# A transformer block on one core: pair 1 by seven block products, z1 of the last tiles behind the change of memory

## The chip, the cores and the metric

The kernel runs on one core of a Trainium2 chip. Its time is the device time of one execution in microseconds. Five engines work side by side, each through its own queue in the order in which the program wrote it: TensorE (PE, matmuls; its weight loads are listed apart as PEld), VectorE (DVE), ScalarE (ACT), GpSimd (POOL) and SyncE (SP), which here issues all DMA transfers. They wait for each other by semaphores.

## The reference

One block on 2048 tokens of width 512, all in float32: a linear-attention half and a gated-MLP half, each behind a layer norm whose scale and shift come from a condition vector `c`.

```python
mod = (silu(c) @ w_mod).reshape(1, 6, 1, -1)          # sa, ca, ga, sb, cb, gb
h = layernorm(x) * (1 + ca) + sa
x = x + ga * A(h, wqkv, wo)                           # linear attention, 32 heads of 16
h = layernorm(x) * (1 + cb) + sb
x = x + gb * B(h, w_in, w_sp, b_sp, w_out)

def B(x, w_in, w_sp, b_sp, w_out):                    # F = 1376, Fh = 688
    z = gelu(x @ w_in)
    z1 = z[..., :Fh]
    z2 = layernorm(z[..., Fh:])
    g = einsum("ts,bsf->btf", w_sp, z2) + b_sp        # 2048 x 2048 by 2048 x 688
    return (z1 * g) @ w_out
```

## The kernel before

Tokens are cut into 16 tiles of 128. Every product is made exact enough by splitting both factors into a high and a low part: the high part is a rounded copy (always on ACT), the low part is the difference (on DVE or POOL), and three matmuls are summed (high by high, high by low, low by high). So each operand costs ACT one pass and DVE or POOL another.

The order of the work is written out by hand. `ORDER` and `ORDER3` are strings of words such as `z013`, operation `z0` for tile 13, and `run_all` (L560) issues them one after the other; each word appends its instructions to the queues of the engines that it uses. What comes earlier in the string comes earlier in each queue. The buffers are chosen by hand as well: `SLOTS` gives for each kind of tile the buffer that its next use takes.

`ORDER` has two parts that flow into each other. The first makes K, Q and the sums of linear attention: weights `wk`, `wq` are built from loaded pieces (`lw` loads, `mr` mean products, `wf` DVE, `qh` high part on ACT, `qd` and `qg` low part on DVE and POOL), x tiles come as they are (`lx`, statistics `s1`) and transposed (`ly`, split by `th`, `tl`), and `kk`, `km`, `qm`, `gm` are the matmuls. The second part works tile by tile: attention output `wo`, residual and statistics `x1`, normalised `h2`, its transpose by DMA (`hp` planes on ACT and transfer, `hm` merge on DVE, `hh`, `hl` split), then two products with `w_in`: `z0` (z1, 24 matmuls of 344 columns, L650) and `z1` (z2, the same), gelu on ACT (`g1`, `g2`), z1 written to memory (in `g1`), z2 normalised (`zl` statistics on DVE with a power op on POOL, `zn` on ACT with its bias `zb` on DVE, L672), parked in memory (`zp`) and split (`zh` on ACT, `zo` on POOL, L686).

Then the memory changes hands: the pools `ws`, `ta`, `tb` and the PSUM pools are closed (L836), and those of the second half are laid over them. `ws` holds `w_in`, so z1 and z2 products come ahead of this point. The last modulation vector (`mB5`, evacuated on ACT at L240) stands directly ahead of it.

`ORDER3` makes `w_sp @ z2`. w_sp is loaded half a row tile at a time (`lh`, 512 KB). Token tiles are taken in pairs. Pairs 2 to 7 use a block scheme that takes seven products in the place of eight: the four blocks of a pair's w_sp give sums (`ss`, DVE, L899 to L908), those are split (`fh` ACT, `fl` DVE, `fg` POOL, L915 and L918), the z2 tiles give differences (`ts` loads the parked z2, `td` DVE) that are split (`th`, `tl`), `pr` p,h,k is one of seven products over eight token tiles (12 matmuls, L928), and `cs`, `cd` add up the results. Pair 0 is done plainly (`aH`, `aL` split w_sp, `pp` t,k is 24 matmuls, `ce` ends). Pair 1 is mixed: its first half (h = 0) by blocks, its second half plainly (`pp2,2 pp2,3 pp3,2 pp3,3`), summed into the same PSUM banks by the table `MIX`.

The result `us` of a tile is multiplied by z1 (`um`, z1 read back by `lz`), cut into 16-bit planes (`up`, two ACT copies), transposed by DMA (`ux`), merged (`ug`, two DVE copies at L278), written to memory (`uq`), read back (`ur`), split (`uh`, `ul`) and multiplied by `w_out` (`wm`, 17 matmuls of 512 columns), and added to the residual (`ot`).

Of the kernel before, what the change touches and what calls it, by code (L numbers as in the profile page):

```python
# [26 lines left out]
def block_kernel(ctx: ExitStack, tc: tile.TileContext, x, x_t, w_qkv, w_o, w_in, w_sp, b_sp, w_out,  # L27
# [641 lines left out]
    def z2_norm(t):  # L669
        z = ZZ[t]  # L670
        b = sm([P, 1], "zb")
        nc.vector.scalar_tensor_tensor(b, MEAN["z", t], -1.0, RSTD["z", t], op0=OP.mult, op1=OP.mult)  # L672
        nc.scalar.activation(z, z, AF.Identity, scale=RSTD["z", t], bias=b)
# [11 lines left out]
    def z2_lo(t):  # L685
        nc.gpsimd.tensor_sub(Z2[t][:, 1], ZZ[t], f(Z2[t][:, 0]))  # L686
# [84 lines left out]
    def hx_lo(t):  # L771
# [19 lines left out]
        yp0,0 yp0,1 wf0,0 wf0,2 kk1,1 kk1,2 yp0,2 kk0,2 kk0,3 lx5 th2 lm0,3 yp0,3 lx2 ya0,1 ya0,2 kk1,3 tl2  # L791
        ya0,3 cr0 qh0,1 qh0,0 qg0,0 lx1 wf0,3 qh0,3 s11 qd0,1 kr0 km2 qh0,2 qg0,2 ce0 bp0 kr1 by0 ly5 s12 kr2
        bp1 qd0,3 bp2 qm0 ba1 by1 by2 ba2 by3 bx1 lo1 th5 qr0 tl5 bp3 ba3 qm1 qr1 bb1 s15 be1 ka0 lM2 ly8 bh2
        bl2 bh0 bl0 k20 k40 km5 k15 qm2 ly3 bx0 lx3 bb0 kh0 kl0 gm0 ka1 th3 tl3 km3 qm3 s13 th8 bh1 bl1 ly4
        lo0 th4 be0 q12 ka2 q22 mV2,0 lx4 mV2,1 ks0 q42 kr3 tl4 k22 k42 km4 k21 k41 li qm5 lw2,0 vh1 ks1 kh1
        q13 ly6 k25 s14 k14 k45 qm4 kh2 ly9 th9 kl2 mS2 kl1 th6 tl6 k24 ka3 mB2 k23 bh3 gm1 tl9 q14 tl8 k43
        bl3 q15 lx6 q24 lx9 ks2 ks3 kh3 qa0 k44 ks4 s16 s19 ks5 lx8 kh4 km8 vh0 wg3 s18 km6 k16 bh9 bh5 bl5
# [375 lines left out]
```

## Time and profile before

| | |
|---|---|
| median of 3 runs | 623.13 us (622.82 to 623.35) |
| the profiled execution's own time | 622.78 us |
| its span, first to last instruction | 621.0 us |
| PE busy | 611.8 us, 3371 matmuls |
| DVE busy | 486.7 us, 907 instructions |
| ACT busy | 334.9 us, 576 instructions |
| POOL busy | 221.5 us, 185 instructions |
| DMA | 105.75 MB, 170 GB/s mean |

The profile is that of one execution. Times are counted from its first instruction. A row of a group reads: line, engine, operation, tiles written and read with their shape, count, then busy us and the mean ns of one, then the engine's idle time just before these instructions and what ended most of it. In a timeline the first two numbers are start and duration in us, and the bracket gives the idle time before it and what released it. Matmuls overlap: each lasts longer than the step from one to the next, so their steps and not their durations tell their cost.

### The profile page before, as it was taken

Reading aid. Unit: us, or ns where it says so; the run is one execution under the profiler, and the core shown is the slowest. Engines: PE = TensorE matmul, PEld = TensorE weight load, DVE = VectorE, ACT = ScalarE, POOL = GpSimd, SP = SyncE. Lnnn points to the kernel's source line nnn. Section 1 sums busy time; section 2 is a strip of 40 time slices with the busy share of each in tenths; the row PEclk is TensorE's granted clock in tenths of the full one; section 3 lists DMA queues with packets and bytes.
Section 4 is the critical chain, followed back from the end, with each engine's and each line's share of the span. In section 5 each row is a group of like instructions: output and inputs, shape, how many; then the busy total and the mean of one; then the engine's idle time right before and its main releaser. Section 6 shows DMA issues by size and latency. Waiting matters only on the chain.

```text
span 621.0 us, 9510 instructions
## 1 busy us (share of the span) xinstructions
PE 611.8 (99%) x3371; PEld 557.5 (90%) x3371; DVE 486.7 (78%) x907; ACT 334.9 (54%) x576; POOL 221.5 (36%) x185
## 2 busy tenths in 40 slices
PE   8999999999999999999999999999999999999997
PEld 6688888888799999999999999999999999998886
DVE  2899989888788988787776599997867786886651
ACT  2778678565556667565536365454454453543420
POOL 0843434635866577364252420232122121300000
PEclk9999999999999999999999999999999999999999
DMA  8454313260244667566734866652586555989962
GB/s 274 155 203 134 103 69 103 65 207 20 84 119 116 164 180 185 173 194 181 209 127 159 316 252 129 203 178 68 172 201 192 150 182 145 288 266 254 292 224 77
DMA packets 91023, 105.75 MB, mean 170 GB/s; under 512 B 57088, under 2 KB 57600, under 8 KB 90976
## 3 DMA queue, kind: packets, MB, share of 16 engines
q1 hardware_dynamic: 90976, 105.15, 56.1%
q8 instruction: 26, 0.43, 0.3%
q14 instruction: 21, 0.17, 0.1%
HBM read 66.07 MB, written 25.95 MB: 148 GB/s over the span
## 4 chain that ended last, share of the span: by engine, by line
PE 83%; DVE 6%; DMA 4%; issue 3%; POOL 1%; SPq 1%; ACT 1%; POOLq 0%; DVEq 0%; ACTq 0%
PE P L928 23%; PE z L650 16%; PE Pq L928 5%; PE pout L112 3%; PE pout L110 3%; PE pout L111 3%; PE kp L111 2%; PE kp L112 2%; PE kp L110 2%; PE g L110 2%; PE g L112 2%; PE g L111 2%; PE qp L112 2%; PE qp L111 2%; PE qp L110 2%
## 5 line engine op out<-in xcount | busy, mean ns | idle before, releaser
L650 PE MATMUL z<-win,ht 128*128 128x344 f32 x768 | 122.9, 320 | 0.2 <-DVE ht L298 0.2
L650 PEld LDWEIGHTS z<-win,ht 128*128 128x128 f32 x768 | 121.4, 188 | 1.3 <-DVE ht L298 0.5
L928 PE MATMUL P<-z,f 128*128 128x344 f32 x624 | 102.7, 320 | 0.0
L928 PEld LDWEIGHTS P<-z,f 128*128 128x128 f32 x624 | 99.0, 188 | 0.1
L918 POOL TENSOR_TENSOR f<-raw_wsp,f 128x512 fp32r<-128x512 f32 x26 | 37.2, 1441 | 138.9 <-ACT f L915 135.5
L254 POOL TENSOR_TENSOR mv<-ve,mhalf 128x1 f32<-128x1 f32 x48 | 36.6, 765 | 58.6 <-DVE ve L253 52.2
L915 ACT ACTIVATE f<-raw_wsp 128x512 fp32r<-128x512 f32 x52 | 31.8, 626 | 29.9 <-PE P L928 14.9
L915 ACT ACTIVATE f<-sa 128x512 fp32r<-128x512 f32 x39 | 24.3, 629 | 34.1 <-DVE sa L905 11.2
L918 DVE TENSOR_TENSOR f<-sa,f 128x512 fp32r<-128x512 f32 x39 | 28.5, 741 | 10.7 <-ACT f L915 10.6
L470 POOL TENSOR_TENSOR pksum<-pksum,tk 128x512 f32<-128x512 f32 x15 | 22.2, 1483 | 40.8 <-DVE tk L442 40.8
L112 PE MATMUL pout<-wout,ut 128*128 128x512 f32 (+1 forms) x85 | 32.4, 382 | 0.0
L110 PE MATMUL pout<-wout,ut 128*128 128x512 f32 (+1 forms) x85 | 32.4, 381 | 0.0
L111 PE MATMUL pout<-wout,ut 128*128 128x512 f32 (+1 forms) x85 | 32.3, 380 | 0.0
L928 PE MATMUL Pq<-z,wsp 128*128 128x344 f32 x192 | 30.9, 322 | 0.9 <-ACT mod L240 0.9
L686 POOL TENSOR_TENSOR z<-zz,z 128x688 fp32r<-128x688 f32 x16 | 28.8, 1817 | 8.0 <-ACT z L683 5.2
L928 PEld LDWEIGHTS Pq<-z,wsp 128*128 128x128 f32 x192 | 30.4, 188 | 1.3 <-ACT mod L240 1.3
L1023 ACT ACTIVATE ut<-ur 128x384 fp32r<-128x384 f32 x32 | 15.3, 518 | 24.2 <-DMA ur<-ud 15.1
L268 ACT COPY uca<-us 128x768 uint16<-128x768 uint16 x32 | 25.0, 828 | 5.2 <-PE P L928 3.6
L579 POOL TENSOR_TENSOR prod<-pq,zrep 128x512 f32<-128x512 f32 x16 | 21.2, 1335 | 15.1 <-ACT zrep L705 4.1
L110 PE MATMUL kp<-wk,ht 128*128 128x512 f32 x64 | 25.8, 403 | 0.0
L111 PE MATMUL kp<-wk,ht 128*128 128x512 f32 x64 | 25.4, 396 | 0.2 <-DVE wk L343 0.2
L110 PE MATMUL g<-pkhl,hhl 128*128 128x512 f32 x64 | 25.3, 396 | 0.0
(257 smaller groups left out, 1546.3 us busy)
## 6 DMA issues: line engine op xcount, KB each, us to landing
raw_wsp<-in_w_sp SPq DMA_DIRECT2D x32, 512.0 KB, 4.7
ud<-uca SPq DMA_DIRECT2D x16, 384.0 KB, 3.4
ur<-ud SPq DMA_DIRECT2D x16, 384.0 KB, 4.1
z1d<-z SPq DMA_DIRECT2D x16, 344.0 KB, 2.3
zd<-zz SPq DMA_DIRECT2D x16, 344.0 KB, 3.0
z1r<-z1d SPq DMA_DIRECT2D x16, 344.0 KB, 3.8
xt<-in_x_t SPq DMA_DIRECT2D x16, 256.0 KB, 3.8
x<-in_x SPq DMA_DIRECT2D x16, 256.0 KB, 2.6
```

The source lines that it names most:

```text
L110: mm(o, a_hi, b_hi, start=first, stop=False, **kw)
L111: mm(o, a_hi, b_lo, start=False, stop=False, **kw)
L112: mm(o, a_lo, b_hi, start=False, stop=last, **kw)
L254: nc.gpsimd.tensor_tensor(mv[:, 1:2], ve, mhalf, op=OP.pow)
L268: nc.scalar.copy(pl[:, h], v[:, :, h])
L470: nc.gpsimd.tensor_add(pksum, pksum, PK[t])
L579: nc.gpsimd.tensor_mul(pr, PQ[t], KV["z"])
L650: mm(p[:, b, :HB], a[:, i, kc], win[h][:, j, kc, b * HB:(b + 1) * HB], start=kc == 0 and k == 0, stop=kc == KC - 1 and k == 2)
L686: nc.gpsimd.tensor_sub(Z2[t][:, 1], ZZ[t], f(Z2[t][:, 0]))
L915: nc.scalar.activation(SF[p, h, k][:, 0], s_src(p, h, k), AF.Copy)
L918: eng.tensor_sub(SF[p, h, k][:, 1], s_src(p, h, k), f(SF[p, h, k][:, 0]))
L928: mm(B[key][:, :HB], a[:, x_], b[:, y_], start=i == 1, stop=i == n)
```

## The change

Five things, and a new `ORDER`, `ORDER3` and `SLOTS` around them.

- The z1 products of tiles 12 to 15 (`z012` to `z015`, `g112` to `g115`) leave `ORDER`. `ORDER3` has `zw` (the same 24 matmuls, into two single banks) and `zg` (gelu in two halves of 344 columns, then the write to memory) in their place.
- Pair 1's second half goes by blocks too: `pp2,2 pp2,3 pp3,2 pp3,3` and their splits go; `ss1,1`, `fh1,1`, `fl1,1`, `fg1,1`, `pr1,1` come, `MIX` goes, and pair 0 uses banks 4 to 7.
- `ug` copies on ACT in the place of DVE.
- `zo`, the low part of z2, is on DVE for tiles 11 to 15.
- The bias `zb` has another form, with one tensor operand in the place of two.

The K weight is loaded in four pieces (`lk`) in the place of two (`lw1`).

```diff
-        nc.vector.scalar_tensor_tensor(b, MEAN["z", t], -1.0, RSTD["z", t], op0=OP.mult, op1=OP.mult)
+        nc.vector.tensor_scalar(b, MEAN["z", t], RSTD["z", t], -1.0, op0=OP.mult, op1=OP.mult)
...
-        nc.gpsimd.tensor_sub(Z2[t][:, 1], ZZ[t], f(Z2[t][:, 0]))
+        (nc.gpsimd if t < 11 else nc.vector).tensor_sub(Z2[t][:, 1], ZZ[t], f(Z2[t][:, 0]))
...
+    def z_late(t):
+        ZB[t, 0] = [bank(2 * (t % 2) + b, f"z0{b}_{t}") for b in range(2)]
+        a = HT2[t]
+        for kc in range(KC):
+            for k, (i, j) in enumerate(((0, 0), (0, 1), (1, 0))):
+                for b in range(2):
+                    mm(ZB[t, 0][b][:, :HB], a[:, i, kc], win[0][:, j, kc, b * HB:(b + 1) * HB],
+                       start=kc == 0 and k == 0, stop=kc == KC - 1 and k == 2)
+
+    def z1_late(t):
+        z = sb("st", [P, 2, HB], F32, f"z1_{t}")
+        for b, p in enumerate(ZB.pop((t, 0))):
+            nc.scalar.activation(z[:, b], p[:, :HB], AF.Gelu_apprx_tanh)
+        Z1D[t] = dram.tile([P, FH], F32, tag=f"z1d{t}", name=f"z1d{t}")
+        dma(Z1D[t], z.rearrange("p a b -> p (a b)"))
...
-    MIX = {(2, 0): ((1, 2), 4, 36), (2, 1): ((1, 3), 5, 36), (3, 0): ((1, 4), 6, 36), (3, 1): ((1, 0), 7, 24)}
-
     def prod(p, h, k):
-        n = 24 if p > 1 else 36 if k in (2, 3, 4) else 12
         for j in range(4):
-            chain((p, k), BANK[k], n, SF[p, h, k][:, :, j], t_of(4 * h + j, k))
+            chain((p, k), BANK[k], 24, SF[p, h, k][:, :, j], t_of(4 * h + j, k))
 
     def plain(t, k):
         for s in range(4):
             for h in range(2):
-                key, where, n = (("q", t, h), 2 * t + h, 3 * NT) if t < QUAD else MIX[t, h]
-                chain(key, where, n, WSP[t, k][:, :, s], Z2[4 * k + s][:, :, h * HB:(h + 1) * HB])
+                chain(("q", t, h), 4 + 2 * t + h, 3 * NT, WSP[t, k][:, :, s], Z2[4 * k + s][:, :, h * HB:(h + 1) * HB])
...
-            if p == 1:
-                nc.vector.tensor_add(U[t1][:, HI], B[p, 0][:, :HB], U[t1][:, HI])
...
-        merge(UC[t][1], UC[t][0].rearrange("p a b -> p (a b)").rearrange("p (a b) -> p a b", b=2))
+        merge(UC[t][1], UC[t][0].rearrange("p a b -> p (a b)").rearrange("p (a b) -> p a b", b=2), nc.scalar.copy)
...
     ORDER = """
-        lm1,0 si lm1,1 du1 du2 du3 du4 cm1,0 cm1,1 lm1,2 lm1,3 lw1,0 cm1,2 cm1,3 mc du5 mr1,0 lw1,1 ly1 th1
-        tl1 ly0 lw0,0 th0 tl0 mr1,1 mr1,2 mr1,3 ce1 wf1,3 qh1,3 mr0,0 lm0,1 lw0,1 mr0,1 mr0,2 mr0,3 qg1,3
-        wf1,1 qh1,1 qg1,1 wf1,0 qh1,0 wf1,2 lx0 s10 qd1,0 kk1,0 qh1,2 qd1,2 lm0,0 kk0,0 kk0,1 lm0,2 ly2 wf0,1
...
+        si lm1,0 lm1,1 du1 du2 du3 du4 cm1,0 cm1,1 lm1,2 cm1,2 lm1,3 cm1,3 lk0 lk1 mc ly0 th0 lk2 tl0 ly1 lk3
+        th1 tl1 du5 mr1,0 mr1,1 mr1,2 mr1,3 ce1 wf1,3 qh1,3 qg1,3 wf1,0 qh1,0 lw0,0 mr0,0 wf1,1 qh1,1 wf1,2
+        qh1,2 lw0,1 lm0,0 mr0,1 mr0,2 mr0,3 yp0,0 qd1,0 lm0,1 yp0,1 lm0,2 wf0,0 lm0,3 yp0,3 kk1,0 qg1,1 kk0,0
+        kk0,1 qd1,2 kk0,2 ya0,1 yp0,2 wf0,2 qh0,2 wf0,1 kk1,1 kk1,2 lx0 kk1,3 ya0,2 ya0,3 ly2 wf0,3 kk0,3
+        qh0,3 qh0,1 th2 s10 kr0 qh0,0 lx2 lx1 s11 kr1 bh0 cr0 tl2 km2 bh1 qg0,0 ce0 li bp3 bp2 bp0 lx5 qg0,2
...
-        aH1,0 aL1,0 hh15 hl15 g213 zl11 z013 g113 zo3 z015 hm14 hh14 hl14 g115 z114 g214 zn11 zp11 zh11 mV5,0
-        mV5,1 mS5 z014 g114 z115 g215 mB5 zo10 zo6
...
+        z112 h215 zh10 zp10 hp15 zo10 x114 hm13 hh13 h214 hl13 g211 hp14 zo7 z113 aH1,0 hm15 hh15 mV5,0 mV5,1
+        hl15 g212 hm14 zh8 zo8 zp3 z115 zl11 g213 hh14 hl14 z114 aL0,0 zn11 zp11 mS5 g215 mB5 zh11 g214 aL1,0
+        zo6
...
     ORDER3 = """
-        zl14 aH0,1 pp1,0 lh2,1 zl12 zn12 aH1,1 zo11 zl13 zn13 lh0,1 zp13 zp12 zl15 aH2,2 aL0,1 aH0,2 zn15 zp15
-        zh15 zh13 zo13 lh1,1 aH0,3 pp0,0 aL2,2 pp2,2 aL0,2 aL1,1 zn14 zh14 aH1,2 aH1,3 pp0,1 aL1,3 zo15 pp0,2
-        zp14 pp1,1 zo14 zh12 zo12 ts3 td3 th3,4 aL1,2 th3,5 ts2 td2 aL0,3 pp0,3 ts1 td1 th1,7 th1,6 lh3,1
...
+        zl13 lh0,1 aH1,1 zw13 zn13 zh13 lh1,1 zg13 aL1,1 aH1,3 zp13 zl12 zn12 zh12 zo13 aH0,1 lh2,0 zl15 zn15
+        zp12 zw12 aL0,1 zg12 zl14 zw15 zn14 aL1,3 pp1,1 zh14 zo14 zp14 zp15 aH0,3 aH1,2 aL1,2 zh15 aH0,2 zo12
+        zo11 zo15 aL0,3 zw14 ts6 td6 th6,6 ts2 th6,5 tl6,6 aL0,2 ts5 td2 th2,4 td5 th5,5 tl5,5 ts3 th6,4 tl6,4
+        td3 th3,5 tl3,5 fh1,0,1 fl1,0,1 ts1 td1 ts0 td0 pp0,3 pp1,3 pp0,1 th2,7 zg14 pp1,2 th0,5 tl0,5 th6,7
...
+        tl7,4 ss2,1,2 um1 up1 pr2,1,2 fh2,0,1 fl2,0,1 ss2,0,3 fh2,0,7 fl2,0,7 ss2,0,1 fh2,1,6 ux1 ug1 uq1
...
+        pr3,0,1 pr3,0,6 fg3,0,2 ux3 ug3 pr3,0,2 fh3,0,4 fg3,0,4 ss3,1,3 fl3,0,7 pr3,0,7 ss3,1,1 fh3,1,5
```

More of the change, by code (lines that the diff above doesn't have):

```diff
@@ L793, in block_kernel @@
[L793 to L797, printed above, removed]
@@ new lines, in block_kernel @@
+        wo3 x13 w02 wo1 q213 wh1,3 wl1,3 wh1,2 wl1,2 h20 ht0 d25 he0 q215 lX2 w12 x12 ap5 h23 z00 am4 ah4 q214
+        al4 h22 hp2 x11 hp3 za0 zb0 wo4 lX6 am5 ah5 al5 wo5 q413 g10 lX4 h21 ht1 g20 d16 hm2 hh2 hl2 z12 hm3
+        d110 he1 d27 d26 g22 x14 h24 z01 z02 hh3 hl3 hp4 q415 z13 d115 g11 d210 g12 d19 q414 ap7 ap6 zl2 lX8
+        x15 g23 hm4 hh4 z11 lX11 hl4 z04 ap10 d18 h25 hp5 am6 z03 g21 ah6 al6 am7 ah7 al7 d29 d28 d111 g14 lX7
+        zl3 d215 zl1 ap8 d211 d114 wo7 x17 z14 zl0 am8 g24 wo6 hm5 hh5 g13 l5 zn0 zp0 hl5 z15 zn1 ah8 ap9 al8
```

177 lines of the change are left out of this document (88 added, 89 removed).

## Prediction, made before the changed kernel ran

> **What bounds the kernel now.** I read the page first, then busy time by stage, then what TensorE (PE) waited for, then the chain.
>
> ```profile
> span 621.0 us, 9510 instructions
> ...
> PE 611.8 (99%) x3371; PEld 557.5 (90%) x3371; DVE 486.7 (78%) x907; ACT 334.9 (54%) x576; POOL 221.5 (36%) x185
> ```
> ```profile
> 20.00:140.00 120.00, 120.00 (x527) 97.46 (x526) 108.31 (x194) 85.65 (x140) 56.30 (x46) 1.00 0.36 119
> 140.00:204.00 64.00, 62.80 (x338) 54.70 (x337) 54.59 (x97) 36.88 (x67) 42.21 (x34) 1.00 0.30 85
> 204.00:334.00 130.00, 129.81 (x769) 124.36 (x768) 101.14 (x209) 75.45 (x123) 68.96 (x60) 1.00 0.63 174
> 334.00:370.00 36.00, 35.09 (x220) 34.66 (x220) 27.23 (x52) 21.60 (x39) 13.38 (x10) 1.00 0.75 273
> 370.00:520.00 150.00, 150.00 (x956) 150.00 (x955) 122.50 (x217) 71.89 (x131) 30.35 (x21) 1.00 0.60 168
> 520.00:540.00 20.00, 19.31 (x120) 18.51 (x119) 17.66 (x29) 8.86 (x16) 4.04 (x3) 1.00 0.69 196
> ```
> ```profile
> PE Pq L928 <- ACT mod L240: 0.9, 1, 0.9
> ...
> PE P L928 <- DVE f L918: 0.5, 1, 0.5
> ```
> ```profile
> 370.04 118.94 PE P L928 x756
> ```
>
> The windows' columns are length, then PE, weight loads, DVE, ACT, POOL (each with its count), clock, DMA share, GB/s. The clock is full throughout. PE has work in every stage; its waits are parts of a microsecond. The chain row gives the pace: 118.94 / 756 = 157.3 ns from one 344-wide product to the next. A matmul that goes is therefore worth 0.157 us if no other engine falls behind, and a microsecond on DVE or ACT is worth nothing until PE waits for it. DVE is the engine nearest to that: 108.31 of 120 us (90%) in the second row, where PE still never stood idle. At 157.3 ns, 20 us hold 127 products; the stage from 520 holds 120, so about 7 x 0.157 = 1.1 us are lost there.
>
> **The start.** The other visible loss is before 20 us.
>
> ```profile
> 16.66 1.98 PE L332 MATMUL wm<-raw_qkv,cbr 128*128 128x512 f32 x4 [0.35 <-DMA raw_qkv<-in_w_qkv]
> ...
> 17.30 0.69 DVE L249 BATCH_NORM_STATS2 bst<-x 128x6 f32<-128x512 f32 x1 [0.75 <-DMA x<-in_x]
> ...
> 18.07 0.79 PE L110 MATMUL kp<-wk,ht 128*128 128x512 f32 x1
> ...
> 18.38 1.28 DVE L343 TENSOR_TENSOR wk<-wf,wk 128x512 fp32r<-128x512 f32 x2
> ...
> 19.11 0.50 PE L111 MATMUL kp<-wk,ht 128*128 128x512 f32 x1 [0.25 <-DVE wk L343]
> ...
> 19.45 0.39 PE L112 MATMUL kp<-wk,ht 128*128 128x512 f32 x1
> ...
> 19.68 0.40 PE L110 MATMUL kp<-wk,ht 128*128 128x512 f32 x1
> ```
>
> The first K matmul starts at 18.07 and the second at 19.11, where the step is otherwise 19.68 - 19.45 = 0.23: 0.8 us go. The second needs the low part of the weight, on DVE at 18.38, and DVE had stood at the statistics of x tile 0, whose load came at 17.30 (`s10` stands ahead of `qd1,0` in the old order). The new order has `qd1,0` and `kk1,0` first and `lx0`, `s10` behind them: 0.8 gone. It also loads `lw0,1` ahead of `lm0,0` and `lm0,1`; before, a 256 KB `lm0,1` stood between the two halves of that weight, and the row at 16.66 waited 0.35 for the second. Together 1.15. The K weight, though, now comes in four 256 KB pieces with x-transpose loads between them on SP, so one mean product may be 0.1 to 0.2 late. I take **-1.0** (ends 0 and -1.2). The matmuls after that need the weight products in the order in which DVE and ACT now make them, so the gain can be carried on.
>
> **The products.** Pair 1's second half was 4 plain calls of 24 matmuls (t = 2, 3 by 8 token tiles by 2 column halves by 3) = 96. It becomes 7 block products of 4 x 3 = 84. The z1 products stay 4 x 24, only later. 12 x 0.1573 = **-1.9 us** on PE (ends 0, if PE waits for the operands instead, and -1.9).
>
> **What the vector engines pay.**
>
> ```profile
> L918 DVE TENSOR_TENSOR f<-sa,f 128x512 fp32r<-128x512 f32 x39 | 28.5, 741 | 10.7 <-ACT f L915 10.6
> ...
> L278 DVE COPY uca<-ucb 128x768 uint16<-128x768 uint16 x32 | 17.5, 603 | 3.5 <-DMA ucb<-uca 3.3
> ...
> L249 DVE BATCH_NORM_STATS2 bst<-zz 128x6 f32<-128x344 f32 x32 | 14.7, 501 | 0.9 <-ACT zz L661 0.9
> ...
> L988 DVE TENSOR_TENSOR us<-us,z1r 128x688 f32<-128x688 f32 x14 | 12.7, 907 | 2.6 <-DMA z1r<-z1d 2.4
> ...
> L899 DVE TENSOR_TENSOR sa<-raw_wsp,raw_wsp 128x512 f32<-128x512 f32 x13 | 9.9, 769 | 7.5 <-DMA raw_wsp<-in_w_sp 5.0 <-issue 2.5
> ...
> L251 DVE BATCH_NORM_AGGREGATE mv<-bst 128x2 f32<-128x6 f32 (+1 forms) x48 | 9.2, 191 | 1.7
> ...
> L672 DVE SCALAR_TENSOR_TENSOR zb<-mv 128x1 f32<-128x1 f32 x16 | 7.4, 462 | 2.6 <-POOL mv L254 2.6
> L253 DVE TENSOR_SCALAR ve<-mv 128x1 f32<-128x1 f32 x48 | 7.4, 154 | 1.7
> ...
> L748 DVE TENSOR_TENSOR wsp<-raw_wsp,wsp 128x512 fp32r<-128x512 f32 x10 | 6.8, 699 | 6.0 <-ACT wsp L745 6.0
> ...
> L965 DVE TENSOR_TENSOR us<-P,c 128x344 f32<-128x344 f32 x7 | 3.5, 505 | 0.1
> ```
> ```profile
> L915 ACT ACTIVATE f<-raw_wsp 128x512 fp32r<-128x512 f32 x52 | 31.8, 626 | 29.9 <-PE P L928 14.9 <-DMA raw_wsp<-in_w_sp 5.6 <-DVE uca L278 3.4
> L268 ACT COPY uca<-us 128x768 uint16<-128x768 uint16 x32 | 25.0, 828 | 5.2 <-PE P L928 3.6 <-DVE uca L278 0.9 <-DMA ud<-uca 0.4
> ```
> ```profile
> L686 POOL TENSOR_TENSOR z<-zz,z 128x688 fp32r<-128x688 f32 x16 | 28.8, 1817 | 8.0 <-ACT z L683 5.2 <-PE Pq L928 2.8
> ```
>
> Of a row's three parts the second is busy us and the mean ns of one. DVE loses the 32 merge copies, 32 x 0.603 = 19.3, two low parts 2 x 0.70 and one add 0.5. It gains four block sums 4 x 0.77 = 3.1, five low parts 5 x 0.74 = 3.7 and the five z2 low parts; a two-input op of that width took 0.907, so 4.5. Net -9.9 us. ACT gains 32 copies; none of this pattern (dense read, spaced write) is in the trace, so I take the mirrored one's 0.828 (ends 0.60, DVE's, and 1.66, twice): 26.5 us, and 3 more high parts (7 less 4), 1.9. ACT had 54% busy, so it has the room. POOL loses 5 x 1.8 = 9.1. The z1 activations in two halves cost ACT some 0.2 us each in its idle time. The zb op in its one-source form should cost L253's 0.15 instead of a mean of 0.46: bounds 0.15 and 1.6. All of this is beside PE, so it counts as 0 unless it makes something late.
>
> The long zb cases show why the form may matter:
>
> ```profile
> 333.54 1.66 POOL L686 TENSOR_TENSOR z<-zz,z 128x688 fp32r<-128x688 f32 x1
> ```
> ```profile
> 333.60 1.61 DVE L672 SCALAR_TENSOR_TENSOR zb<-mv 128x1 f32<-128x1 f32 x1 [0.73 <-POOL mv L254]
> ```
>
> A one-column op lasted 1.61 us and ended with POOL's op. [...]
>
> **Behind the change of memory.** The first late product waited 0.9 for the evacuation of the last modulation tile (L240). The first z1 product (`zw13`) opens the same two banks (2 and 3) right behind the same `mB5`, so I keep that wait: 0 (ends -0.9, and +0.7 with another gelu ahead on ACT). What the z1 products buy is time for z2. Until `pp0,3`, which needs the last four z2 tiles, PE has four z1 products and `pp1,1`: 5 x 24 x 0.1573 = 18.9 us. In that time DVE has four statistics (2 x 0.50 + 0.19 + 0.15 = 1.35) 5.4, four zb 0.6, five z2 low parts 4.5 and five low parts of w_sp 3.5, 14.0 us, and some 2 us of waiting for POOL's power op (0.73 in the row at 333.60, up to four times, 2.9 at most). 16 to 17 against 18.9: covered by 2 us. Ahead of it, 4 x 24 x 0.1573 = 15.1 us of PE work leave the stage from 204; DVE's 101.1 us, less 4 for zb, then stand against 115 us: 84%, under the 90% that cost nothing earlier.
>
> SP gets four z1 writes of 344 KB behind the change. They wait for the gelus, and what is queued behind them waits too:
>
> ```profile
> SPq L657 <- ACT z L655: 11.1, 3, 5.2
> ```
>
> Two of the four stand ahead of the first transfers of t operands, two behind; 1.4 MB at the 273 GB/s of that stage is 5 us of transfer where a quarter of 36 us was free. I count 0, and 0 to +2 as ends.
>
> **Where the merges stood in the way.**
>
> ```profile
> 519.82 0.69 DVE L899 TENSOR_TENSOR sa<-raw_wsp,raw_wsp 128x512 f32<-128x512 f32 x1 [2.93 <-DMA raw_wsp<-in_w_sp]
> ...
> 534.01 1.09 DVE L278 COPY uca<-ucb 128x768 uint16<-128x768 uint16 x2 [0.65 <-DMA ucb<-uca]
> ...
> 535.00 0.67 DVE L918 TENSOR_TENSOR f<-sa,f 128x512 fp32r<-128x512 f32 x1
> ```
> ```profile
> DMA to landing us min/median/max: 3.6/4.0/6.3
> ```
>
> At 534 DVE waited for a DMA transpose (second fence: issue to landing), copied 1.09, and only then made the low part that PE waited for. That cause goes; the late w_sp load at 519.82 may stay. I take **-0.6** of the 1.1 lost (ends 0, -1.1). On ACT the same wait now holds the high parts queued behind a merge, and PE waits for those; in the new order `ux1 ug1` and `ux3 ug3` stand side by side. For that, and for a rearranged order of everything, I add **+0.5**, the wait of P for DVE f once more (ends 0 and +6, what the first rival prices).
>
> **Sum**, on the profiled execution's 622.78 us (span 621.0): -1.0 - 1.9 - 0.6 + 0.5 = -3.0, so 619.8. That execution lies 0.35 below the median of the runs shown, 623.13, which would give 620.1; I say **619.8**.
>
> **Rivals.**
> 1. *The vector chain doesn't follow* (the slower one). Place: the stage from 204, where 15.1 us of PE work leave while DVE's work stays. DVE was idle for 28.9 us there. It has to close 15.1 - 4 = 11 of them; what it can't close, because it stood waiting for ACT, POOL and transposes, becomes PE idle time. The new kernel is slower when more than 4.7 of the 11 us stay (3.5 of gain and the 1.25 that tell). At 6 of 11: 622.8 - 3.5 + 6 = 625.3. For it: the stage is a chain through five queues. Against: 90% without a PE wait from 20 to 140.
> 2. *ACT takes DVE's place.* Sixteen merges can wait 4.0 us for a transpose with high parts behind them. DVE did so three times (3.3 us) and it reached PE once (0.5). Half of sixteen at 0.5 is 4 us less ACT's lead: +1 to +3, so 620.5 to 622.5. Against: ACT is idle 52% from 370 to 520.
> 3. *The shorter product list buys nothing*, since pair 1's four extra sums and seven splits make DVE the bound there: -1.9 falls away and the start remains: 621.7 to 622.5.
>
> **Chances.** The forecast (617.5 to 621.3) 0.58; rival 1 0.15; rival 2 0.17; rival 3 0.10. About 0.2% (1.25 us) is what a measurement can tell from no change: below 621.9 is faster, above 624.4 slower. Rival 2 splits 0.10 faster, 0.05 same, 0.02 slower; rival 3 0.03 and 0.07. That gives faster 0.71, same 0.12, slower 0.17. The range, 616.6 to 625.2, takes in all start and stall gains at their far ends (622.8 - 1.2 - 1.9 - 1.1 - 0.9 = 617.7, and a microsecond for waits from 140 to 204 that a new order may close) and reaches rival 1's time; outside it I leave 0.06 below and 0.12 above.
>
> **What would show it.** Right: matmul count down by 12 to 3359; the second K matmul 0.23 us behind the first, and the last K matmul of tiles 0 and 1 about 1 us earlier; L278 of uca on ACT near 830 ns; zb near 150 ns with none over 1 us; the wait for L240 before the first `z` product still near 0.9; PE idle below 0.3 us from there to 520. Wrong: PE rows under 99% in the windows ahead of the change of memory (rival 1), waits of P for ACT f (rival 2), waits of P for DVE f or t between the z1 products and pair 2 (rival 3), or a first K matmul after 18.1 us.

## The result and the profile after

The changed kernel takes 625.26 us (median of 22 runs, 622.95 to 626.81), the kernel before 623.16 beside it: a ratio of 1.0029, with an interval of 1.0018 to 1.0040. It is slower by about 1.8 us, where 3 us of gain were forecast; the time lies just above the range. The profiled run took 626.01. The first lines of its page:

```profile
span 624.2 us, 9491 instructions
...
PE 614.2 (98%) x3359; PEld 557.8 (89%) x3359; DVE 473.9 (76%) x886; ACT 364.9 (58%) x615; POOL 214.0 (34%) x180
```

There are 12 matmuls fewer, as meant, and PE is nonetheless busy 2.4 us longer. Busy time by stage, with the columns of the prediction's table, cut where the stages now end:

```profile
20.00:140.00 120.00, 119.82 (x526) 97.07 (x525) 107.62 (x197) 84.58 (x138) 56.23 (x47) 1.00 0.35 108
140.00:204.00 64.00, 61.15 (x314) 52.57 (x313) 53.27 (x90) 34.40 (x62) 40.24 (x32) 0.97 0.35 105
204.00:323.00 119.00, 118.19 (x693) 112.43 (x692) 93.00 (x211) 73.73 (x123) 68.20 (x59) 1.00 0.68 179
323.00:370.00 47.00, 46.31 (x292) 45.88 (x291) 39.07 (x82) 25.36 (x49) 3.49 (x5) 1.00 0.66 232
370.00:520.00 150.00, 149.14 (x940) 147.35 (x940) 110.06 (x178) 90.51 (x151) 33.99 (x23) 1.00 0.58 163
```

The second row is the odd one: in 64 us PE has 314 matmuls, where it had 338 before, it stands idle for 2.85 us, where it was 1.2, and the mean clock is 0.97. What PE waited for, in the view of the waits (total us, times, longest):

```profile
PE tpp L308 <- POOL pq L594: 1.3, 1, 1.3
...
PE z L653 <- ACT z L658: 0.8, 1, 0.8
PE po L115 <- POOL pt L301: 0.8, 1, 0.8
PE z L863 <- ACT mod L243: 0.7, 1, 0.7
PE P L947 <- DVE f L937: 0.5, 1, 0.5
PE pkv L722 <- DVE gh L131: 0.5, 1, 0.5
```

The fourth and fifth are the two of before (line numbers have moved by 3 to 19), and the sixth was there as well, with 0.4. The first three are new, and all of them lie ahead of the change of memory. The place is shown by the last matmul ahead of that point, first in the kernel before, then in the changed one:

```profile
334.21 0.40 PE L238 MATMUL pmod<-yl,ones 128*128 128x512 f32 x1
335.51 0.74 PE L928 MATMUL Pq<-z,wsp 128*128 128x344 f32 x3 [0.91 <-ACT mod L240]
```
```profile
323.19 0.40 PE L241 MATMUL pmod<-yl,ones 128*128 128x512 f32 x1
324.27 0.90 PE L863 MATMUL z<-win,ht 128*128 128x344 f32 x4 [0.69 <-ACT mod L243]
```

96 z1 products have gone from the stretch ahead of it, 96 x 0.1573 = 15.1 us, so 319.1 was due, and less by what the start gained. It came at 323.19: 4.1 us late. Behind it lie 624.2 - 323.2 = 301.0 us, before 621.0 - 334.2 = 286.8: 14.2 more, where 15.1 - 1.9 = 13.2 were due, so 1.0 us is lost there. Together 4.1 + 1.0 - 1.9 = 3.2, the difference of the spans. The 4.1 is what the experiments trace. The 1.0 is no firm loss: seven profiled runs of kernels that are alike behind this point (the changed kernel and six of the experiments) take from 300.0 to 302.8 us for that part.

**Where the 4 us went.** Timeline of the changed kernel around 150 us (start and duration in us; the bracket is the idle time before and its releaser):

```profile
145.23 3.45 DVE L713 TENSOR_SCALAR bz<-zrep,colv 128x128 f32<-128x128 f32 x4 [0.52 <-ACT zrep L708]
145.27 1.30 POOL L582 TENSOR_TENSOR prod<-pq,zrep 128x512 f32<-128x512 f32 x1 [3.70 <-ACT zrep L708]
...
146.53 1.68 POOL L533 TENSOR_TENSOR win<-raw_win,win 128x688 fp32r<-128x688 f32 x1
...
150.20 0.40 PE L241 MATMUL pmod<-yl,ones 128*128 128x512 f32 x1
...
150.82 1.06 POOL L594 TENSOR_TENSOR pq<-pq,den 128x512 f32<-128x512 f32 x1 [2.61 <-DVE den L592]
...
151.93 0.66 PE L308 MATMUL tpp<-ident,pq 128*128 128x128 f32 x4 [1.33 <-POOL pq L594]
...
153.08 0.39 PE L722 MATMUL pkv<-gh,wv 128*128 128x256 f32 x1 [0.49 <-DVE gh L131]
```

and of the kernel before:

```profile
146.25 1.82 DVE L710 TENSOR_SCALAR bz<-zrep,colv 128x128 f32<-128x128 f32 x4
...
150.00 1.06 POOL L591 TENSOR_TENSOR pq<-pq,den 128x512 f32<-128x512 f32 x1
...
152.23 0.39 PE L719 MATMUL pkv<-gh,wv 128*128 128x256 f32 x1 [0.44 <-DVE gh L128]
...
155.04 0.62 PE L305 MATMUL tpp<-ident,pq 128*128 128x128 f32 x4
```

The words of this stage: `vb` makes the bias rows, `d1` and `d2` scale a tile of q by its divisor (`d12` and `d22` for tile 2: `prod` and `pq` on POOL, `den` on DVE), `at` transposes it, `gh` splits a quarter of the sum G, `kv` are the products with it, `mB` is a modulation product. Two words of the new order meet here. `at2`, the transposes of the scaled q, stood behind `kv2` and began at 155.04, four us after their operand was ready; it now stands ahead of `kv0` and is due at 150.4. And `wl0,1`, the low part of a w_in piece, now follows `d12` on POOL: the four bias rows on DVE, 1.82 us before, take 3.45 beside it, so that the chain den, pq behind them ends at 151.88 and not at 151.06. The longest of the four rows lasts 1.71 beside POOL's 1.68, the two that no POOL operation overlaps 0.27 and 0.28. PE waits 1.33 us, then 0.49 for the split of G, whose DVE operations stand in the same queue.

Then the clock. Two stretches of the changed kernel, with the columns of the table by stage:

```profile
150.00:153.40 3.40, 1.58 (x10) 0.91 (x8) 2.94 (x5) 3.16 (x7) 2.58 (x2) 1.00 0.35 136
153.40:157.00 3.60, 3.60 (x21) 3.60 (x20) 2.69 (x6) 1.50 (x4) 3.60 (x4) 0.55 0.00 0
```

PE was busy for 1.58 of 3.40 us, and in the stretch that follows the granted clock is 0.55: in the trace's record of the clock it is 0.5 from 153.76 on for 3.41 us. That costs half of 3.41, 1.7 us. Of the 22 runs of the changed kernel 7 have a mean clock of 0.997 or less (3.41 us at half of 624 are 0.003; two of the 7 show 0.994, twice that); their median is 626.23, that of the 15 others 624.06. Of the 117 runs of the kernel before beside the experiments below, 1 has.

### The profile page after: what moved, and what is told of

Read it like the earlier page. It is cut to its first block, busy times and chain, and to the rows that moved or that the text cites. A ratio compares the mean times of both kernels' runs of the same rounds, so it can differ in the third digit from the quotient of the medians.

```text
span 624.2 us, 9491 instructions
## 1 busy us (share of the span) xinstructions
PE 614.2 (98%) x3359; PEld 557.8 (89%) x3359; DVE 473.9 (76%) x886; ACT 364.9 (58%) x615; POOL 214.0 (34%) x180
## 4 chain that ended last, share of the span: by engine, by line
PE 80%; DVE 8%; DMA 5%; ACT 3%; issue 2%; POOL 1%; ACTq 0%; DVEq 0%; POOLq 0%
PE P L947 17%; PE z L653 16%; PE Pq L947 5%; DMA ucb<-uca 3%; PE pout L115 3%; PE pout L114 3%; PE pout L113 3%; PE z L863 2%; PE g L113 2%; PE g L115 2%; PE g L114 2%; PE po L115 2%; PE qp L115 2%; PE qp L114 2%; PE qp L113 2%; PE po L114 2%
## 5 line engine op out<-in xcount | busy, mean ns | idle before, releaser
L947 PE MATMUL P<-z,f 128*128 128x344 f32 x672 | 111.0, 321 | 0.3
L653 PE MATMUL z<-win,ht 128*128 128x344 f32 x672 | 108.0, 320 | 0.8 <-ACT z L658 0.8
L653 PEld LDWEIGHTS z<-win,ht 128*128 128x128 f32 x672 | 106.4, 188 | 2.0 <-ACT z L658 1.1
L947 PEld LDWEIGHTS P<-z,f 128*128 128x128 f32 x672 | 106.5, 188 | 1.5 <-DVE f L937 1.2
L937 POOL TENSOR_TENSOR f<-raw_wsp,f 128x512 fp32r<-128x512 f32 x28 | 42.1, 1515 | 172.9 <-ACT f L934 153.7
L937 DVE TENSOR_TENSOR f<-sa,f 128x512 fp32r<-128x512 f32 x42 | 31.2, 749 | 21.2 <-ACT f L934 21.1
L934 ACT ACTIVATE f<-raw_wsp 128x512 fp32r<-128x512 f32 x56 | 34.2, 624 | 14.2 <-PE P L947 8.0
L281 ACT COPY uca<-ucb 128x768 uint16<-128x768 uint16 x32 | 31.9, 1065 | 13.4 <-DMA ucb<-uca 13.2
L937 DVE TENSOR_TENSOR f<-raw_wsp,f 128x512 fp32r<-128x512 f32 x28 | 23.7, 854 | 9.7 <-ACT f L934 9.5
L115 PE MATMUL po<-m,pt 128*128 128x512 f32 x64 | 25.5, 398 | 0.8 <-POOL pt L301 0.8
L113 PE MATMUL kp<-wk,ht 128*128 128x512 f32 x64 | 25.8, 403 | 0.2 <-ACT tk L434 0.2
```

What stands on the lines that cost most here:

```text
L113: mm(o, a_hi, b_hi, start=first, stop=False, **kw)
L115: mm(o, a_lo, b_hi, start=False, stop=last, **kw)
L281: copy(o[:, :, h], plt[:, h * n:(h + 1) * n].rearrange("p a b -> p (a b)"))
L653: mm(p[:, b, :HB], a[:, i, kc], win[h][:, j, kc, b * HB:(b + 1) * HB], start=kc == 0 and k == 0, stop=kc == KC - 1 and k == 2)
L934: nc.scalar.activation(SF[p, h, k][:, 0], s_src(p, h, k), AF.Copy)
L937: eng.tensor_sub(SF[p, h, k][:, 1], s_src(p, h, k), f(SF[p, h, k][:, 0]))
```

## The experiments

Theory 1: the loss is the stage at 150 us, the wait of `at2` and the clock behind it. Rivals: the other new waits (POOL's `pt` at 191.5, ACT's gelu at 251), the merges on ACT, and those of the prediction. Medians are given with the ratio to the kernel before on the same chip.

### The collision on POOL alone

```diff
-        vb q113 lW1,0 d12 wl0,1 d22 gm14
+        vb q113 lW1,0 d12 d22 wl0,1 gm14
```

> The changed kernel with one word moved: `wl0,1` (low part of a w_in piece, POOL, L533) goes behind `d22`, so that POOL doesn't work beside the bias rows of DVE (L713) and ahead of `d22`. Theory 1 (the time is lost where the transposes `at2`, now ahead of `kv0`, wait 1.3 us for POOL's pq, and in the half-rate clock window that follows): the bias rows take 1.8 us again in the place of 3.45, pq is ready some 1.6 us earlier, PE's step at 150.2 has no wait above 0.3, no run shows a granted clock under 1.000, and the median falls by 2 to 3.5 us, to 621.8 to 623.3. Rival (the loss is the sum of later waits on ACT and POOL): the wait moves to the next product, and the median stays within 0.8 us of the changed kernel's 625.3.

Measured: 624.37 (1.0019, 1.0007 to 1.0031), and all 12 runs at a clock of 0.999 or more. The wait of the transposes is gone (timeline, then waits):

```profile
145.44 2.01 DVE L713 TENSOR_SCALAR bz<-zrep,colv 128x128 f32<-128x128 f32 x4 [0.52 <-ACT zrep L708]
...
150.70 0.65 PE L308 MATMUL tpp<-ident,pq 128*128 128x128 f32 x4
```
```profile
PE pkv L722 <- DVE gh L131: 1.5, 2, 1.0
```

The bias rows are short again, pq is ready in time, the half clock is away. But a microsecond came back at once: the last product of kv waits 1.0 for the last piece of G's split, which stands behind `d20` in DVE's and ACT's queue. So a part of theory 1 holds, and the gain is 0.9 by the medians and 0.6 by the ratios, whose intervals overlap, and not 2 to 3.5.

### The whole stage

```diff
-        gh0 mS4 gh1 d10 gh2 d13 d11 lW0,2 wh0,2 mB3 at2 d20 gh3 d23 kv0
+        gh0 mS4 gh1 d10 gh2 gh3 d13 d11 lW0,2 wh0,2 mB3 at2 d20 d23 kv0
```

on top of the edit above.

> e1_pool with one more word moved: `gh3` (last piece of the split G, ACT and DVE) goes from behind `d20` to behind `gh2`, since e1_pool still waited 1.36 us there, at the last product of kv (`kv3`). If the stage of kv is the whole difference to the kernel before: this wait goes too, the half clock stays away, and the median falls from e1_pool's 624.4 to 622.5 to 623.3. If the wait passes on to the products behind it (`pm`, which wait for kv's mask and split on DVE and ACT): the sum of the waits from 150 to 165 us falls by under 0.6 and the median stays within 0.4 of e1_pool.

Measured: 623.23 (1.0001, 0.9992 to 1.0010), all 12 runs at 0.999 or more. Two words moved give back 2.0 us by the medians, 1.7 by the ratios, all of what was lost against before. Theory 1 holds for the difference of the two kernels; the gains of the forecast are still missing, so more was lost than that.

### The two waits behind it

```diff
-        xp_lo(f"p{t}", PT[t], nc.gpsimd)
+        xp_lo(f"p{t}", PT[t], nc.vector if t == 5 else nc.gpsimd)
...
-        za0 zb0 wo4 lX6 am5 ah5 al5 wo5 q413 g10
+        za0 zb0 wo4 lX6 am5 ah5 q413 al5 wo5 g10
...
-        zh1 hp8 h26 hp6 g15 zo4
+        zh1 hp8 g15 h26 hp6 zo4
```

The cause of the second of them, in the changed kernel:

```profile
247.21 1.68 POOL L689 TENSOR_TENSOR z<-zz,z 128x688 fp32r<-128x688 f32 x1
247.51 1.93 DVE L263 SCALAR_TENSOR_TENSOR h<-xr,mv,mod 128x512 f32<-128x512 f32 x1 [1.05 <-DMA x1d<-xr]
...
250.31 1.14 ACT L271 COPY xph<-h 128x512 uint16<-128x512 uint16 x2 [3.98 <-issue]
...
251.35 1.37 ACT L658 ACTIVATE z<-z 128x688 f32<-128x688 f32 x2
...
252.14 0.58 PE L653 MATMUL z<-win,ht 128*128 128x344 f32 x2 [0.81 <-ACT z L658]
```

`h` on DVE takes 1.93 us beside POOL's operation, where the median of its kind is 0.74, and comes late; ACT stands for 3.98 us ahead of the planes made of it, and the gelu queued behind them frees PE's banks too late. The gelu needed none of this; it only stood behind.

> The changed kernel with its two long waits between 180 and 260 us mended: the low part `al5` on DVE in the place of POOL and behind `q413`, and the gelu `g15` ahead of the planes `hp6` on ACT. If those two waits (1.15 us at 191.5, 1.1 at 251.0) are lost time on PE's path: both vanish and the median falls by 1.8 to 2.3 us, to 623.0 to 623.5, with the clock still under 1.000 in about a third of the runs. By theory 1 alone (the transposes and the clock carry the loss, and these waits are slack that other waits take up before the change of memory): at most 0.8 us of fall.

Measured, without the stage at 150 mended: 625.0 (1.0020, 1.0003 to 1.0036), 5 of 12 runs with the half clock. Both waits are gone from the profile (steps of 0.2 and 0.5 us are left), and yet the median is only 0.3 lower than the changed kernel's, by the ratios 0.6. The interval of this one is too wide to say more.

> e5_kv and e2_zstage together: the stage of kv mended, and the two waits at 191 and 251 us. If the waits of PE ahead of the change of memory are what the change lost, and add up: the start's 0.7 and the products' 1.9 are left as gain, less 0.4 for waits behind it, and the median is 620.8 to 622.3, below the kernel before (623.3). If waits mended here are given back in the second half (its own waits for w_sp loads and transposes decide): 623 to 624.5.

Measured, with the stage at 150 mended too: 621.85 (0.9972, 0.9960 to 0.9984; 6 runs), faster than both kernels. Against e5_kv that is 1.4 us by the medians and 1.8 by the ratios, for waits of 2.3 us, so there they add up. The windows of this kernel ahead of the change of memory, which now comes at 318.3:

```profile
140.00:204.00 64.00, 62.97 (x337) 54.47 (x336) 54.08 (x96) 36.27 (x65) 42.09 (x34) 1.00 0.38 111
204.00:318.00 114.00, 114.00 (x668) 108.52 (x667) 88.70 (x204) 72.02 (x120) 65.77 (x57) 1.00 0.68 183
```

PE stands idle for nothing from 204 to 318 us, with 15 us of z1 products taken away. In the six profiled runs of kernels with both places mended (this one and the five built on it) the last modulation product stands at 318.30 to 318.79, where 319.1 less the start's gain was due. So what was lost ahead of the change of memory is accounted for. It is still not the forecast: of its 3.0 us e6_all gains 1.3 by the medians and 1.7 by the ratios, and where the rest went is open. The nearest candidate, which no run tests, is that PE in its profile stands idle for 1.4 us from 370 to 520, where it stood for nothing before.

### The start

The old order there: `lx0 s10` ahead of `qd1,0`, `lm0,0 lm0,1` ahead of `lw0,1`; `lx0` and `s10` go from their later places (not shown).

```diff
-        qh1,2 lw0,1 lm0,0 mr0,1 mr0,2 mr0,3 yp0,0 qd1,0 lm0,1 yp0,1
+        qh1,2 lm0,0 lm0,1 lw0,1 mr0,1 mr0,2 mr0,3 yp0,0 lx0 s10 qd1,0 yp0,1
```

> The changed kernel with the old order at the start: the load and statistics of x tile 0 (`lx0 s10`) ahead of `qd1,0`, and `lm0,0 lm0,1` ahead of `lw0,1`. By the forecast's first term the first K matmuls come about 1 us later, at 18.1 to 18.6, and the median rises by 0.7 to 1.0 us, to 626.0 to 626.3. Rival (the start is not on the path: a wait further on absorbs it): the first matmuls are later, but the bound at 150 us and the median do not move by more than 0.3.

Measured: 626.18 (1.0052, 1.0033 to 1.0071; 6 runs, 3 of them with the half clock), 0.9 above the changed kernel by the medians and 1.4 by the ratios, and at 150 us it is 1.1 late. The intervals of the two kernels overlap, so the size is loose; the direction is that of the forecast. In the changed kernel the start looks like this:

```profile
17.39 0.80 PE L113 MATMUL kp<-wk,ht 128*128 128x512 f32 x1
18.02 0.40 PE L114 MATMUL kp<-wk,ht 128*128 128x512 f32 x1
18.26 0.39 PE L115 MATMUL kp<-wk,ht 128*128 128x512 f32 x1
```

The second matmul stands 0.63 us behind the first, and no wait is shown there. It does so in all 13 profiled runs with the new start (0.63 to 0.64); in the five with the old start, this one among them, it is 1.02 to 1.55. The place of the first matmul says less: in the 13 it lies anywhere from 16.40 to 17.49.

### Twelve matmuls put back

On e6_all, one block product of pair 1 twice:

```diff
-        for j in range(4):
-            chain((p, k), BANK[k], 24, SF[p, h, k][:, :, j], t_of(4 * h + j, k))
+        for j in list(range(4)) * (2 if (p, h, k) == (1, 1, 1) else 1):
+            chain((p, k), BANK[k], 36 if (p, k) == (1, 1) else 24, SF[p, h, k][:, :, j], t_of(4 * h + j, k))
```

> e6_all with one block product of pair 1 (`pr1,1,1`, 12 matmuls) issued twice, which adds it twice to the result: the twelve matmuls that the change saves are put back as work of PE alone, with no operand more. By the forecast's term (12 x 0.1573): the median rises by 1.9 us, to 623.5 to 624.0. If PE there waits for DVE or ACT in any case, so that matmuls saved are worth nothing: under 0.7 us of rise.

Measured: 623.73 (0.9996, 0.9981 to 1.0011), 1.88 above e6_all by the medians and 1.5 by the ratios. That fits the term of 12 x 0.1573; the runs lie from 621.66 to 624.29, so its size is not known to a tenth.

### The merges on DVE again

```diff
-        merge(UC[t][1], UC[t][0].rearrange("p a b -> p (a b)").rearrange("p (a b) -> p a b", b=2), nc.scalar.copy)
+        merge(UC[t][1], UC[t][0].rearrange("p a b -> p (a b)").rearrange("p (a b) -> p a b", b=2))
```

> The changed kernel with the merges `ug` on DVE again (L281), all else as it is. If ACT's merges (1.07 us each in this direction, two of them behind a transfer) cause the waits of P for f at 422 to 432 and 504 us: these waits go and the median falls by 1 to 2 us. If DVE is the nearer engine there, as the forecast had it: DVE's 19 us of copies come back, new waits of P for DVE f appear, and the median rises by 0.6 to 4 us. Theory 1 has no say on it beyond the stage before the change of memory, which should stay as it is.

Measured: 638.44 (1.0250, 1.0231 to 1.0270; 5 runs), 13 us above the changed kernel, far beyond both expectations. Its waits:

```profile
PE P L947 <- DVE f L937: 3.8, 6, 1.2
PE pout L113 <- DVE us L971: 3.2, 1, 3.2
```

The place of the merges is right, and it is no small matter in this order: DVE's queue holds its low parts so close that 19 us of copies between them reach PE many times over, half clock included (0.991 to 0.995 in four of five runs).

### z1 back ahead of the change of memory

`z0` and `g1` of tiles 12 to 15 beside their z2 products; three of the z1 results in `st` buffers.

> The changed kernel with the z1 products of tiles 12 to 15 back ahead of the change of memory, each beside its z2 product (`z0`, `g1`), and none in the second order; three of the four z1 results go through the `st` buffers that hold w_sp halves. By the forecast's reason for the move (15 us of PE work cover the z2 chain of the last four tiles, 16 to 17 us): PE stands still 8 to 13 us ahead of `pp0,3`, and the time is 632 to 638. Rival (their place does not matter, since the z2 chain ends in time behind the other products): within 2 us of the changed kernel.

Measured, one run: 640.85, at a mean clock of 0.986. PE's waits behind the change of memory:

```profile
PE Pq L947 <- ACT wsp L748: 7.8, 2, 5.3
PE Pq L947 <- DVE wsp L751: 1.5, 1, 1.5
PE Pq L947 <- DVE z L689: 1.4, 1, 1.4
```

10.7 us of waits, in the range that was expected, and clock lost behind them, so that the time lies above the 632 to 638. But the z2 tiles are only 1.4 of it; most is for the high parts of w_sp on ACT. The z1 products cover both. How much of ACT's 7.8 is due to the edit itself, whose z1 results hold buffers that w_sp loads want, is left open.

### The banks at the change of memory

On e6_all: the PSUM banks of the second half are laid out in the order of their numbers.

```diff
+    for k in range(8):
+        bank(k, f"lay{k}")
     dma(bsp, b_sp)
```

> e6_all with one addition: the eight PSUM banks of the second half are laid out in the order of their numbers before any is used, so that the first z1 product (`zw13`, banks 2 and 3) lies over the banks of the attention output and no longer over those of the last modulation tile. By the forecast's reading (the wait of about 1 us at the change of memory is that of two reused banks for the evacuation at L243): the step of 1.08 us between the last modulation matmul and the first z1 product falls under 0.2, and the median falls by 0.7 to 1.1 us to 620.7 to 621.2. Rival (the product also waits for something else there, or the time is taken up by the z2 chain behind it): the median stays within 0.4 of e6_all's 621.85.

Measured: 621.88 (0.9974, 0.9962 to 0.9987), the same as e6_all. The wait itself went as expected:

```profile
318.79 0.39 PE L241 MATMUL pmod<-yl,ones 128*128 128x512 f32 x1
319.02 1.27 PE L865 MATMUL z<-win,ht 128*128 128x344 f32 x7
```

from a step of 1.08 us to one of 0.23. It was not worth anything: in this profile PE has steps of 0.92 at 372.7 and 0.54 at 377.0, where e6_all has one of 0.43 at 376.6 and 0.157 is the pace. The reading of the wait was right, its price was not.

### The two small edits

On e6_all, `zb` in its old form and all low parts of z2 on POOL; then each alone.

```diff
-        nc.vector.tensor_scalar(b, MEAN["z", t], RSTD["z", t], -1.0, op0=OP.mult, op1=OP.mult)
+        nc.vector.scalar_tensor_tensor(b, MEAN["z", t], -1.0, RSTD["z", t], op0=OP.mult, op1=OP.mult)
...
-        (nc.gpsimd if t < 11 else nc.vector).tensor_sub(Z2[t][:, 1], ZZ[t], f(Z2[t][:, 0]))
+        nc.gpsimd.tensor_sub(Z2[t][:, 1], ZZ[t], f(Z2[t][:, 0]))
```

> e6_all with the two small edits undone: the bias `zb` in its form with two tensor operands, and the low part of z2 on POOL for all tiles. If these two keep the z2 chain of the last tiles short behind the change of memory, as the forecast had it (covered by only 2 us): POOL's 1.8 us for each low part and zb's up to 1.6 us lie in that chain, PE waits 1 to 5 us ahead of `pp0,3`, and the median is 622.8 to 627. If both lie beside other work: within 0.4 us of e6_all's 621.85.

> e6_all with the bias `zb` alone back in its form with two tensor operands. e11_small undid both small edits and lost 2.9 us. If the form is the part that matters (a one-column operation held for up to 1.65 us beside POOL's low parts): the median is over 623 here and under 622.5 with the other edit alone undone.

> e6_all with the low part of z2 alone back on POOL for all tiles. If the place of the low parts is what e11_small's 2.9 us measured (five of 1.8 us in POOL's queue ahead of the low parts that POOL makes for the first block products): the median is 623.5 to 625 here, and within 0.6 of 621.85 with the form of `zb` alone undone.

Measured: both undone 624.70 (1.0023, 1.0010 to 1.0036), 2.85 above e6_all; the form of `zb` alone 622.20 (0.9976), no difference; the low parts alone 623.99 (1.0002, 0.9991 to 1.0014), by the ratios 1.9 us. It is the low parts. First a POOL row, then a DVE group from 318 to 365 us, both of e14_zo, then the same group of e6_all:

```profile
332.09 7.76 POOL L689 TENSOR_TENSOR z<-zz,z 128x688 fp32r<-128x688 f32 x4 [2.14 <-ACT z L686]
```
```profile
L751 DVE TENSOR_TENSOR wsp<-raw_wsp,wsp 128x512 fp32r<-128x512 f32 x6 | 6.1, 1022 | 4.9 <-ACT wsp L748 4.9
```
```profile
L751 DVE TENSOR_TENSOR wsp<-raw_wsp,wsp 128x512 fp32r<-128x512 f32 x6 | 4.1, 686 | 2.3 <-ACT wsp L748 2.3
```

While POOL works through four low parts, DVE's operations beside it are stretched, 686 to 1022 ns, and PE pays for it not ahead of `pp0,3`, where it was expected, but at 368 to 379 us, in four waits for t operands and low parts that DVE makes next. These four steps lie 1.7 us over the pace in e14_zo and 2.5 in e11_small, where e6_all has one of 0.3.

### The half clock

The stage put into the kernel before: `vb` ahead of `d12`, `wl0,1` behind it, `at2` ahead of the kv products; with `mB4` behind `kv2` in the second, and `gh0` behind `gh2` in the third.

> The kernel before with the one suspect arrangement put in: `vb` ahead of `d12`, `wl0,1` straight behind `d12` on POOL, and the transposes `at2` ahead of `mB4` and `kv0`. Theory 1: DVE's bias rows stretch to over 3 us beside POOL, PE waits 1 to 2 us for pq, the granted clock falls to half for one window in some of the runs (under 1.000 in the list), and the median rises by 1 to 4 us over 623.2. Rival (such a wait is caught up by the slack up to the change of memory, and the half clock comes from elsewhere): no run under 1.000 and a median within 0.6 us of the kernel before.

> The kernel before with the whole suspect stage: as e4_before_gap, and `mB4` behind `kv2`, so that behind the transposes PE waits a second time, for the split of G, as in the changed kernel (1.7 and 0.6 us within 2.5 us there). If two waits so close bring the half clock, as they did in 7 of 22 runs of the changed kernel and in none of 12 of e4_before_gap with 1.6 and 0.24: part of the runs show a clock of 0.997 or less, and the median is 625 to 627. If the half clock has another cause in the changed kernel: all runs at 0.999 or more, and a median at e4_before_gap's 624.7 within 0.6.

> e10_before_gap2 with the first piece of G's split (`gh0`) behind `gh2`, since there the second wait did not come about: now PE waits 1.6 us for pq and then some 0.5 us for the split. If two waits so close bring the half clock: part of the runs at 0.997 or less and a median of 625 to 627. If not: all at 0.999 or more, and 624.4 to 625.2, by the second wait alone.

Measured: 624.69 (1.0029, 1.0016 to 1.0042), 624.35 (1.0015, 1.0004 to 1.0026) and 625.29 (1.0026, 1.0015 to 1.0037). The wait for pq appears in all three (1.2 us, a step of 1.62) and the medians rise by 1.1 to 1.6 us: such a wait is not caught up further on. But the second wait did not come about in any of them, since G's split was done while PE waited for pq, and none of the 36 runs shows the half clock. In e4_before_gap PE was busy 2.05 of the 3.4 us:

```profile
150.00:153.40 3.40, 2.05 (x11) 1.24 (x10) 2.26 (x5) 2.37 (x5) 3.37 (x3) 1.00 0.52 172
153.40:157.00 3.60, 3.60 (x31) 3.51 (x31) 2.35 (x6) 1.61 (x4) 3.14 (x4) 1.00 0.00 0
```

The other way round, in the changed kernel, PE was given work that nobody needs while it waits:

```diff
         p = ps("t", [P, KC, P], "tp" + key)
+        for i in range(16 if key == "p2" else 0):
+            mm(p[:, i % KC, :], ones, ones, start=True, stop=True)
```

> The changed kernel with 16 matmuls of the constant `ones` (128 columns each), written into the bank of the transposes `at2` directly ahead of them and overwritten by them: PE works while it waits for POOL's pq, and nothing else is changed. If the half clock comes from PE standing idle there: all runs at 0.999 or more, and the median falls to that of the changed kernel's runs at full clock, 624.1, within 0.6. If it has another cause: a third of the runs stay at 0.997 or less, and the median stays at 625.3.

Measured: 623.82 (0.9997, 0.9986 to 1.0008), all 12 runs at 0.999 or more; the first window after 150 us has PE busy for most of it, the second runs at full clock:

```profile
150.00:153.40 3.40, 3.11 (x28) 2.88 (x27) 3.27 (x6) 2.96 (x6) 3.15 (x3) 1.00 0.21 80
153.40:157.00 3.60, 3.60 (x30) 3.47 (x29) 2.39 (x6) 1.61 (x4) 3.36 (x4) 1.00 0.00 0
```

The half clock comes from PE's idle time there; with the fill the median is 1.4 us lower, by the ratios 2.0. The records of the clock in the profiles of the changed kernel and the kernel before show what stood ahead of it. In both the clock changes only at whole multiples of 3.413 us from the first entry (43, 44 and 181 of them in the changed kernel, 181 in the kernel before), and that entry lies at 6.99 and 4.65 us. Counted in windows of that grid, PE was busy for 1.59 us in the one from 150.35 of the changed kernel and for nothing in the one in which each program ends, and half clock followed these three; in all other windows of the two at full clock it was busy for 2.27 us or more, and half clock followed none.

That would also explain the third of the runs. From the start of the first wait to the end of the second it is 2.48 us (150.60 to 153.08), so a window of 3.41 holds both in 0.93 of its 3.41 possible places: 27%, an estimate, for 7 of 22 runs. It supposes that the grid may lie anywhere against the program and that half clock follows only a window with both waits. Four other profiles have the same two waits, 1.3 and 0.5 us: e2_zstage, e3_merge and e7_start, each with a mean clock of 1.000, and e8_z1back with 0.986, in which its other waits may have a part.

## Why the prediction was wrong

- **Start, -1.0**: right in mechanism and nearly in size. The first K matmul came 0.68 earlier, the second 1.09, the bound at 150 us 0.73 (149.97 for 150.70), and undoing it costs 0.9 to 1.4. The second matmul came 0.63 behind the first and not 0.23, with no wait between them: of the 0.8 that was read as DVE's delay only 1.04 - 0.63 = 0.41 was one. With the 0.35 of the weight load that makes 0.76.
- **Products, -1.9**: right (1.5 to 1.9 for twelve put back). Rival 3, that they buy nothing, falls.
- **Merges, -0.6**: the place was right, the sizes were not. The copy takes 1065 ns on ACT and not the mirrored one's 828 (within the ends of 0.60 and 1.66):

```profile
L281 ACT COPY uca<-ucb 128x768 uint16<-128x768 uint16 x32 | 31.9, 1065 | 13.4 <-DMA ucb<-uca 13.2
```

  From 520 to 540 PE no longer stands idle, as forecast (0.69 us before). But from 370 to 520 it now stands for 0.86, where it stood for nothing, waiting for DVE's low parts at 423 to 433. ACT stood 13.2 us for the transposes, and still PE waited for no high part itself, so the sign of rival 2 is missing; whether the merges are behind those low parts, which are made from ACT's high parts, is open. Taken off DVE the merges are worth 13 us in this order, which was built around it; what they gain against the kernel before no run shows.
- **Low parts of z2 and zb at 0**: wrong for the low parts, nearly 2 us in this order. The prediction counted the length of the five on each engine; it did not ask what POOL's five would hold up on DVE. For `zb` the 0 is right: the mean fell from 462 to 203 ns, and it moves no time.
- **The wait at the change of memory kept at 0.9**: right (0.69, a step of 1.08), and without value, as e9_banks shows.
- **+0.5 for a rearranged order**: this is the step that failed; with the words put right, the loss becomes a gain of 1.3 to 1.7 (e6_all). It was priced by one wait, that of P for DVE f, in the stage where the change was said to be. The new `ORDER` also rearranged stages that the five named things do not touch, and there it cost 4.8 us in the profiled run: 323.19 against 334.21 - 15.1 - 0.73 = 318.4. By the steps of PE the transposes, the first kv product and the products behind kv account for 1.0, the half clock for 1.7 (in a third of the runs, the profiled one among them), the waits at 191 and 251 us, less two of before at 192 and 204, for 1.6; the other 0.5 lies in smaller steps. Both words of the first collision, `wl0,1` ahead of `d22` and `at2` ahead of `kv0`, could be read in the order beside the row of `pq` that the profile of before holds.
- **Rival 1** named 625.3, which is the time that came, by luck and not for its reason. It put the loss in the stage from 204, where the z1 products leave, because the vector chain could not close up. e6_all has the same products gone and PE busy for 114.00 of 114.00 us there. The chain closes up; words stood at wrong places.
- **z1 products as cover for z2**: they are needed (e8_z1back), and more for w_sp's high parts on ACT than for z2, which the forecast had not counted.

## What to carry to other kernels

When an order written by hand is replaced, each word that moved ahead of another on any engine is a change of its own: look up when its operand was ready in the old profile, and what the word now ahead of it in that queue waits for. Two PE gaps close to each other, 1.8 us together, cost their length and, in 7 of 22 runs, some 1.7 us more by the clock behind them, so one of them was worth filling (1.4 us by the medians), while another gap of 1.08 us, once closed, gave nothing: the run decides. Where only some runs lose time, look at the clock record of several traces before choosing a cause. A place in a single profile can differ by a us between two runs of the same code, as their times do (621.99 to 624.62 in 22 runs of the kernel before), so a term of that size needs runs and not one pair of profiles. An operation taken off one engine is to be priced by what it held up on another, not by its own length only.

## What the runs showed of the hardware

- **A clock halved behind two short waits.** Two waits of PE, 1.33 and 0.49 us with four transposes between, were followed by 3.41 us at half clock in the profile of the changed kernel. The window of 3.413 us ahead of it held 1.59 us of work, as the profile counts it, so it was not idle; with 2.27 us or more in such a window, in this profile and that of the kernel before, the clock stayed full. With the first wait filled in e16_fill all 12 runs were at 0.999 or more. What follows a window with between 1.59 and 2.27 us of work, these two profiles do not show.
- **Rows with one tensor operand were stretched beside POOL.** Four bias rows (one tensor and one column) took 3.45 us in the changed kernel, where POOL's operations overlapped two of them (1.43 and 1.71), 1.82 in the kernel before, where one was overlapped (1.23), and 2.01 in e1_pool, where POOL's next operation came behind them; in the profiles of the two kernels a row that none overlapped took 0.27 to 0.28. `zb` in its form with one tensor operand was not: it took 0.21 us within an operation of POOL of 1.81, and never over 215 ns.
- **A merge cost ACT more than a split.** Dense read and spaced write took 1065 ns in the changed kernel, spaced read and dense write of the same size 828 in the kernel before and 830 in the changed one.
